# Attention followed by a low-rank mixer: two sets of TensorE transposes replaced by crossbar DMA, u^T in tiles, and the sequence mixer one step later

## The chip, the cores and the metric

The kernel runs on one core of one Trainium2 chip. The metric is device time in microseconds (us). PE is TensorE's matmul part, PEld its weight loads, DVE is VectorE, ACT ScalarE, POOL GpSimd, SP SyncE (here it only issues DMAs). A run over 1.5% above the fastest of its kernel is called slow and left out of the ratios.

## The reference, cut to what matters

```python
# q, k, v: (8 batches, 8 heads, 576 tokens, 64); causal attention with a decay bias from cumsum(max(s, 0))
x  = attention(q, k, v, s)                  # (8, 576, 512)
h  = x.transpose(0, 2, 1) @ U @ V           # low-rank mix over the tokens, rank 32
u  = x + h.transpose(0, 2, 1)               # "sequence mixer"
out = u + np.maximum(u @ w_ch1, 0) @ w_ch2  # "channel mixer", 512 -> 2048 -> 512
```

## The kernel before: the parts that matter

Attention runs over 32 steps `n`, each of two heads of one batch (4 steps a batch). The work is written as Python generators. At each `yield` of an attention or sequence-mixer generator, the driver inserts one piece of channel mixer as *filler* for TensorE. One channel-mixer group has 512 tokens and 32 pieces; a piece is four matmuls of 512 columns. `pace` skips some of the slots.

The sequence mixer of one batch computes `U^T x`, casts it on DVE, and then accumulates, per 128 channels, the transposed x (identity matmuls) and `V^T (U^T x)` into the same tile of PSUM (the memory that matmuls write), so that u^T comes out:

```python
def seqmix(b):                               # cut
    for t in range(5): matmul(up, lhsT=U_sb[:, t, :], rhs=x_sb[:, t, :])
    nc.vector.tensor_copy(ux, up)            # 128x512 cast; the V matmuls need it
    yield
    for dt in range(4):
        for t in range(4):                   # x transposed on TensorE
            matmul(ut[:, ds(t*128, 128)], lhsT=x_sb[:, t, ds(dt*128, 128)], rhs=identity, ...)
        matmul(ut, lhsT=ux[:, ds(dt*128, 128)], rhs=V_sb[:, 0:512], ...)
        copy(uT[:, dt, ds(b*S, 512)], ut)
        yield
    ...                                      # the last 64 tokens, in the same way
def chanmix(g):                              # cut
    for nf in range(16): ...                 # 4 matmuls of 512 columns, ReLU on ACT, yield
    for i in range(4):
        ...                                  # 16 matmuls of 512 columns into f2, yield after each 4
        for dt in range(4):                  # residual: u back to token rows on TensorE
            matmul(f2[:, ds(dt*128, 128)], lhsT=uT[:, dt, ds(tok, 128)], rhs=identity, ...)
        nc.vector.tensor_copy(o_sb, f2)      # then stored
for n in range(PB, NP + 1):                  # the main loop; PB = 4, NP = 32
    ...                                      # transposes(n+1), scores(n), values(n-1), each with filler
        if hp == 0:                          # first step of batch b: mixer of batch b-1
            run(seqmix(b - 1)); fill.append(chanmix(b - 1)); pace[1] = 7   # 7 of 8 slots filled
```

The softmax here doesn't subtract the row's maximum and nothing guards it: scores larger than these inputs give would overflow.

## Time and profile before

The first lines are from the profile's page: the busy table, and the chain of waits that ended last.

```profile
PE 394.9 (96%) x3659; PEld 229.0 (56%) x3659; DVE 222.7 (54%) x445; ACT 199.6 (49%) x384; POOL 56.5 (14%) x79
...
PE 84%; DVE 5%; DMA 4%; ACT 4%; POOL 1%; issue 1%; ACTq 0%
PE pwork L399 30%; PE pwork L412 28%; PE pscore L252 9%; PE pwork L313 6%; PE pwork L231 3%; DMA v_slot_102<-in_v_dram 2%; PE pwork L336 2%; PE pwork L423 2%; PE pwork L357 2%; PE pwork L349 2%; DMA slot_94<-rows_hbm 1%; DVE x_sb L323 1%; PE pscore L149 1%; POOL v_slot_102 L190 1%; DMA hT<-in_s_dram 1%
```

TensorE has nearly all of the span and 84% of the chain. The identity matmuls, L423 (residual) and L349 (x transposed), stand with 2% each on the chain. The next lines are the stretch view, from one sequence mixer's start to the next: length, busy time (and count) of PE, PEld, DVE, ACT and POOL, granted TensorE clock (1.00 is full speed), DMA share (the time of all packets over that of 16 engines; it can pass 1), GB/s.

```profile
129.59:172.59 43.00, 43.00 (x437) 25.67 (x435) 28.23 (x54) 22.09 (x44) 5.88 (x7) 1.00 0.77 69
172.59:215.56 42.97, 42.97 (x436) 25.62 (x434) 27.65 (x54) 22.08 (x44) 5.88 (x7) 1.00 0.70 69
```

PE has no idle time at all there, at full clock. What leaves PE's queue leaves the span, as long as no other wait takes its place.

What does an identity matmul cost? The group table gives 219 ns for each, but matmuls overlap in the pipeline. Start times are the better measure. The timeline (start, length, engine, line, operation, count) at the end of the span:

```profile
401.64 1.67 PE L412 MATMUL pwork<-w_sb,hT 128*128 128x512 bf16 x7
403.15 0.39 PE L423 MATMUL pwork<-identity,uT 128*128 128x128 bf16 x4
403.37 3.62 PE L412 MATMUL pwork<-w_sb,hT 128*128 128x512 bf16 x16
406.82 0.39 PE L423 MATMUL pwork<-identity,uT 128*128 128x128 bf16 x4
```

Four identity matmuls hold PE from 403.15 to 403.37, 0.22 us; sixteen of 512 columns take 3.45 us, 215.6 ns each. The Trainium skill ("TensorE: Matmul & The Clock Gate", section "Wait — 56ns, not 53.3ns?") has N/2.4 GHz + 2.5 ns start to start once the clock is warm, 55.6 and 215.7 ns for 128 and 512 columns. This trace agrees. I use that below as the *slot* of a matmul (at least 25 ns), and call what is left between two starts a *gap*.

### The profile page before, as it was taken

Reading aid. Unit: us, or ns where it says so; the run is one execution under the profiler, and the core shown is the slowest. Engines: PE = TensorE matmul, PEld = TensorE weight load, DVE = VectorE, ACT = ScalarE, POOL = GpSimd, SP = SyncE. Lnnn points to the kernel's source line nnn. Section 1 sums busy time; section 2 is a strip of 40 time slices with the busy share of each in tenths; the row PEclk is TensorE's granted clock in tenths of the full one; section 3 lists DMA queues with packets and bytes.
Section 4 is the critical chain, followed back from the end, with each engine's and each line's share of the span. In section 5 each row is a group of like instructions: output and inputs, shape, how many; then the busy total and the mean of one; then the engine's idle time right before and its main releaser. Section 6 shows DMA issues by size and latency. Waiting matters only on the chain.

```text
span 411.3 us, 8682 instructions
## 1 busy us (share of the span) xinstructions
PE 394.9 (96%) x3659; PEld 229.0 (56%) x3659; DVE 222.7 (54%) x445; ACT 199.6 (49%) x384; POOL 56.5 (14%) x79
## 2 busy tenths in 40 slices
PE   7798989989999999999999999999999999999996
PEld 3475446646565566555655556555656555444442
DVE  7774036866665666665667556676656544002011
ACT  5552688526742574338631873078416830530610
POOL 6750053200500050005000310000000000000000
PEclk9759999999999999999999999999999999999999
DMA  5999999950891059103921195000010001001002
GB/s 75 167 209 208 150 133 122 150 68 29 102 103 54 28 77 128 46 34 48 130 59 53 24 144 66 27 30 3 26 53 27 2 27 51 27 26 56 23 26 77
DMA packets 59301, 29.68 MB, mean 72 GB/s; under 512 B 42302, under 2 KB 53598, under 8 KB 59262
## 3 DMA queue, kind: packets, MB, share of 16 engines
q0 software_dynamic: 53360, 18.44, 62.9%
q1 hardware_dynamic: 5902, 10.69, 7.6%
q8 instruction: 28, 0.46, 0.5%
q14 instruction: 11, 0.09, 0.1%
HBM read 37.51 MB, written 9.95 MB: 115 GB/s over the span
## 4 chain that ended last, share of the span: by engine, by line
PE 84%; DVE 5%; DMA 4%; ACT 4%; POOL 1%; issue 1%; ACTq 0%
PE pwork L399 30%; PE pwork L412 28%; PE pscore L252 9%; PE pwork L313 6%; PE pwork L231 3%; DMA v_slot_102<-in_v_dram 2%; PE pwork L336 2%; PE pwork L423 2%; PE pwork L357 2%; PE pwork L349 2%; DMA slot_94<-rows_hbm 1%; DVE x_sb L323 1%; PE pscore L149 1%; POOL v_slot_102 L190 1%; DMA hT<-in_s_dram 1%
## 5 line engine op out<-in xcount | busy, mean ns | idle before, releaser
L406 ACT ACTIVATE hT<-pwork 128x512 bf16<-128x512 f32 x144 | 88.1, 612 | 133.5 <-PE pwork L399 132.6
L412 PE MATMUL pwork<-w_sb,hT 128*128 128x512 bf16 x576 | 143.2, 379 | 0.2 <-DMA q_sd<-in_q_dram 0.2
L399 PE MATMUL pwork<-uT,w_sb 128*128 128x512 bf16 x576 | 141.0, 379 | 0.5 <-ACT slot_96 L237 0.3
L412 PEld LDWEIGHTS <-hT 128*128 128x128 bf16 x576 | 52.0, 98 | 46.5 <-issue 0.3
L399 PEld LDWEIGHTS <-w_sb 128*128 128x128 bf16 x576 | 51.0, 98 | 46.4 <-issue 0.7
L432 DVE COPY o_sb<-pwork 128x512 f32<-128x512 f32 x36 | 24.9, 692 | 65.4 <-PE pwork L423 65.2
L263 ACT ACTIVATE pT_86<-pscore 128x512 bf16<-128x512 f32 x32 | 19.3, 604 | 32.9 <-PE pscore L252 32.8
L323 DVE TENSOR_TENSOR x_sb<-pwork,rec 128x320 bf16<-128x320 f32 x64 | 31.4, 491 | 2.1
L97 POOL DMA_DIRECT2D q_sd<-in_q_dram x10 | 8.3, 827 | 164.1 <-PE pwork L231 148.2
L366 DVE CAST uT<-pwork 128x512 bf16<-128x512 f32 x30 | 20.5, 690 | 14.2 <-PE pwork L357 14.2
L322 DVE RECIPROCAL rec<-pwork 128x5 f32<-128x5 f32 x64 | 12.3, 192 | 24.7 <-PE pwork L313 24.5
L237 DVE COPY slot_96<-pwork 64x576 bf16<-64x576 bf16 x22 | 17.4, 797 | 13.6 <-PE pwork L231 13.3
L264 DVE TENSOR_TENSOR pT_86<-pT_86,keep 128x512 bf16<-128x512 bf16 x32 | 13.3, 415 | 20.7 <-ACT pT_86 L263 20.7
L264 DVE TENSOR_TENSOR pT_87<-pT_87,keep 128x512 bf16<-128x512 bf16 x32 | 13.2, 415 | 20.1 <-ACT pT_87 L263 20.0
L276 ACT ACTIVATE pT_86<-pscore 128x512 bf16<-128x512 f32 x32 | 19.5, 611 | 5.2 <-PE pscore L252 5.1
L263 ACT ACTIVATE pT_87<-pscore 128x512 bf16<-128x512 f32 x32 | 19.4, 607 | 5.3 <-PE pscore L252 5.2
L231 PEld LDWEIGHTS <-q_sd 72*128 72x128 bf16 x256 | 15.8, 100 | 11.1 <-DMA q_sd<-in_q_dram 0.9
L313 PEld LDWEIGHTS <-pT_87 128*128 128x128 bf16 x480 | 18.8, 100 | 5.6 <-DVE pT_87 L289 0.4
L237 DVE COPY slot_93<-pwork 64x576 bf16<-64x576 bf16 x26 | 20.6, 797 | 1.7 <-PE pwork L231 1.2
L231 PE MATMUL pwork<-identity,k_sd 72*128 72x72 bf16 x256 | 19.1, 201 | 2.2 <-DVE pT_86 L289 1.3
L313 PEld LDWEIGHTS <-pT_86 128*128 128x128 bf16 x480 | 18.5, 100 | 4.5 <-issue 0.6
L276 ACT ACTIVATE pT_87<-pscore 128x512 bf16<-128x512 f32 x32 | 19.6, 612 | 2.9 <-PE pscore L252 2.8
(98 smaller groups left out, 480.2 us busy)
## 6 DMA issues: line engine op xcount, KB each, us to landing
out_dram<-o_sb SPq DMA_DIRECT2D x36, 256.0 KB
w_sb<-in_moe_w_ch_dram POOLq DMA_DIRECT2D x2, 2048.0 KB, 20.6
q_sd<-in_q_dram POOLq DMA_DIRECT2D x7, 576.0 KB, 8.8
k_sd<-in_k_dram POOLq DMA_DIRECT2D x7, 576.0 KB, 12.6
v_slot_102<-in_v_dram POOLq DMA_DIRECT2D x12, 128.0 KB, 13.0
v_slot_103<-in_v_dram POOLq DMA_DIRECT2D x12, 128.0 KB, 13.1
v_slot_104<-in_v_dram POOLq DMA_DIRECT2D x8, 128.0 KB, 12.6
rows_hbm<-hT SPq DMA_DIRECT2D x1, 504.0 KB
```

Source lines behind the costliest of these rows:

```text
L231: nc.tensor.transpose(tp[:, c, t2, :], src[:, h, ds(t2 * 128, 128)], identity[:TP, :TP])
L237: copy(dst[:, :, :, :, par], tp[par * D : par * D + D].rearrange("p c t m -> p c m t"),)
L252: nc.tensor.matmul(dst, lhsT=kT[:, ds(j * 128, 128)], rhs=qT[:, lo:hi], start=True, stop=True,)
L263: nc.scalar.activation(pT[:, hh, 0:512], diag, EXP, scale=scale)
L264: nc.vector.tensor_tensor(pT[:, hh, 0:512].rearrange("p (a b) -> p a b", a=4), pT[:, hh, 0:512].rearrange("p (a b) -> p a b", a=4), keep.t ...
L276: nc.scalar.activation(pT[:, hh, 512:1024], far, EXP, scale=scale)
L313: nc.tensor.matmul(po[:, i, :], lhsT=pT[:, hh, ds(place(j, i), 128)], rhs=vt[:, j, h, :], start=(j == 0), stop=(j == i), skip_group_check= ...
L323: nc.vector.tensor_tensor(x_sb[:, :, ds(h * D, D)], po[:, :, 0:D], rec.to_broadcast([128, 5, D]), op=ALU.mult,)
L399: nc.tensor.matmul(f1, lhsT=w1_sb[:, kt, ds(nf * 128, 128)], rhs=uT[:, kt, ds(g * 512, 512)], start=(kt == 0), stop=(kt == 3),)
L406: nc.scalar.activation(hT[:, nf, :], f1, RELU)
L412: nc.tensor.matmul(f2, lhsT=hT[:, nf, ds(i * 128, 128)], rhs=w2_sb[:, nf, :], start=(nf == 0), stop=False, skip_group_check=True,)
L432: nc.vector.tensor_copy(o_sb, f2)
```

## The change

The intent: take the x transposes (batches 2 to 7) and all residual matmuls off TensorE. Both transposes go to the DMA crossbar (a DMA that transposes while it copies); the additions join PSUM evacuations that DVE does anyway. For that, u^T is kept in one tile per token group, x is stored by head pair, and from batch 2 on the mixer runs one step later, to give the last transpose of a batch time to land. The diff, cut to its core:

```diff
+    FT = 2
-    uT = consts.tile([128, 4, B * S], BF16)
+    def uT(g): ...  # work.tile([128, 4, 512], BF16, tag="uT", bufs=4), one per token group
 def values(n):
-            x_of[b] = work.tile([128, 5, DM], BF16, ...)
+            x_of[b] = work.tile([128, PB, 5, 128], BF16, ...)
+            if b >= FT: xT_of[b] = work.tile([128, 4, 640], BF16, tag="xT", bufs=1)
...
+            if hh == 1 and b >= FT:
+                nc.sync.dma_start_transpose(
+                    out=xT_of[b][:, hp, :].rearrange("p (t m) -> p t m", t=5),
+                    in_=x_sb[:, hp, :, :].rearrange("p t d -> p (t d)"))
 def seqmix(b):
+        def evac(dt, lo, hi, src):           # cut where a token group ends
+            if xT is not None: nc.vector.tensor_tensor(dst, src, xT[:, dt, lo:hi], op=ALU.add)
+            ...                              # else a copy, as before
...                                          # identity matmuls only if xT is None
 def chanmix(g):
+        u_sd = work.tile([128, 4, 4, 128], BF16, tag="u_sd")
+        nc.sync.dma_start_transpose(out=u_sd..., in_=u...)    # 512 KB, all of the group
...
-            for dt in range(4): nc.tensor.matmul(f2[:, ds(dt * 128, 128)], lhsT=uT[...], rhs=identity, ...)
-            nc.vector.tensor_copy(o_sb, f2)
+            nc.vector.tensor_tensor(o_sb..., f2..., u_sd[:, :, i, :], op=ALU.add)
 main loop
-    for n in range(PB, NP + 1):
+    for n in range(PB, NP + 2):
...
+        if hp == 1 and b > FT:
+            run(seqmix(b - 1))
+            fill.append(chanmix(b - 1))
-            if hp == 0:
+            if hp == 0 and b <= FT:
```

More of the change, by code (lines that the diff above doesn't have):

```diff
@@ L210, with uT @@
     load_v(1)
-    uT = consts.tile([128, 4, B * S], BF16)
-    x_of = {}
+    uT_of, x_of, xT_of = {}, {}, {}
+    def uT(g):
+        if g not in uT_of:
+            uT_of[g] = work.tile([128, 4, 512], BF16, tag="uT", name="uT", bufs=4)
+        return uT_of[g]
     def transposes(n):
@@ L305, in values @@
         if hp == 0:
-            x_of[b] = work.tile([128, 5, DM], BF16, tag="x_sb", name="x_sb")
+            x_of[b] = work.tile([128, PB, 5, 128], BF16, tag="x_sb", name="x_sb")
+            if b >= FT:
+                xT_of[b] = work.tile([128, 4, 640], BF16, tag="xT", name="xT", bufs=1)
         x_sb, pT, vt = x_of[b], pTs[n % 2], v_slots[b % 3]
@@ L323, in values @@
             nc.vector.tensor_tensor(
-                x_sb[:, :, ds(h * D, D)],
+                x_sb[:, hp, :, ds(hh * D, D)],
                 po[:, :, 0:D],
@@ L328, in values @@
             )
+            if hh == 1 and b >= FT:
+                nc.sync.dma_start_transpose(
+                    out=xT_of[b][:, hp, :].rearrange("p (t m) -> p t m", t=5),
+                    in_=x_sb[:, hp, :, :].rearrange("p t d -> p (t d)"),
+                )
             yield
@@ L338, in seqmix @@
                 lhsT=U_sb[:, t, :],
-                rhs=x_sb[:, t, :],
+                rhs=x_sb[:, :, t, :],
                 start=(t == 0),
@@ L345, in seqmix @@
         yield
+        xT = xT_of.pop(b, None)
+        cut = 512 - 64 * b
+        def evac(dt, lo, hi, src):
+            g, at = (b, 64 * b + lo) if lo < cut else (b + 1, lo - cut)
+            dst = uT(g)[:, dt, at : at + hi - lo]
+            if xT is not None:
+                nc.vector.tensor_tensor(dst, src, xT[:, dt, lo:hi], op=ALU.add)
+            elif b == 0 and type(dt) is int and dt % 2:
+                nc.scalar.copy(dst, src)
+            else:
+                nc.vector.tensor_copy(dst, src)
         for dt in range(4):
             ut = pwork()
-            for t in range(4):
+            if xT is None:
+                for t in range(4):
+                    nc.tensor.matmul(
+                        ut[:, ds(t * 128, 128)],
+                        lhsT=x_sb[:, dt, t, :],
+                        rhs=identity,
+                        start=(t == 0),
+                        stop=False,
+                        skip_group_check=True,
+                    )
+            nc.tensor.matmul(
+                ut,
+                lhsT=ux[:, ds(dt * 128, 128)],
+                rhs=V_sb[:, 0:512],
+                start=(xT is not None),
+                stop=True,
+                skip_group_check=True,
+            )
+            evac(dt, 0, cut, ut[:, 0:cut])
+            if cut < 512:
+                evac(dt, cut, 512, ut[:, cut:512])
+            yield
+        ut = pwork()[:, 0:256].rearrange("p (a b) -> p a b", a=4)
+        for dt in range(4):
+            if xT is None:
                 nc.tensor.matmul(
-                    ut[:, ds(t * 128, 128)],
-                    lhsT=x_sb[:, t, ds(dt * 128, 128)],
-                    rhs=identity,
-                    start=(t == 0),
+                    ut[:, dt, :],
+                    lhsT=x_sb[:, dt, 4, :],
+                    rhs=identity[:, :64],
+                    start=True,
                     stop=False,
@@ L357, in seqmix @@
             nc.tensor.matmul(
-                ut,
+                ut[:, dt, :],
                 lhsT=ux[:, ds(dt * 128, 128)],
-                rhs=V_sb[:, 0:512],
-                start=False,
+                rhs=V_sb[:, 512:S],
+                start=(xT is not None),
                 stop=True,
@@ L364, in seqmix @@
             )
-            copy = nc.scalar.copy if b == 0 and dt % 2 else nc.vector.tensor_copy
-            copy(uT[:, dt, ds(b * S, 512)], ut)
-            yield
-        ut = pwork()
-        for dt in range(4):
-            nc.tensor.matmul(
-                ut[:, ds(dt * 64, 64)],
-                lhsT=x_sb[:, 4, ds(dt * 128, 128)],
-                rhs=identity[:, :64],
-                start=True,
-                stop=False,
-                skip_group_check=True,
-            )
-            nc.tensor.matmul(
-                ut[:, ds(dt * 64, 64)],
-                lhsT=ux[:, ds(dt * 128, 128)],
-                rhs=V_sb[:, 512:S],
-                start=False,
-                stop=True,
-                skip_group_check=True,
-            )
-        nc.vector.tensor_copy(
-            uT[:, :, ds(b * S + 512, 64)], ut[:, 0:256].rearrange("p (a b) -> p a b", a=4)
-        )
+        evac(slice(0, 4), 512, S, ut)
         yield
@@ L395, in chanmix @@
         hT = work.tile([128, NF, 512], BF16, tag="hT", name="hT")
+        u = uT_of.pop(g)
+        u_sd = work.tile([128, 4, 4, 128], BF16, tag="u_sd", name="u_sd")
+        nc.sync.dma_start_transpose(
+            out=u_sd.rearrange("p a b c -> p (a b) c"), in_=u.rearrange("p a b -> p (a b)")
+        )
         for nf in range(NF):
@@ L401, in chanmix @@
                     lhsT=w1_sb[:, kt, ds(nf * 128, 128)],
-                    rhs=uT[:, kt, ds(g * 512, 512)],
+                    rhs=u[:, kt, :],
                     start=(kt == 0),
@@ L409, in chanmix @@
             f2 = pwork()
-            tok = g * 512 + i * 128
             for nf in range(NF):
@@ L416, in chanmix @@
                     start=(nf == 0),
-                    stop=False,
-                    skip_group_check=True,
+                    stop=(nf == NF - 1),
                 )
@@ L421, in chanmix @@
                     yield
-            for dt in range(4):
-                nc.tensor.matmul(
-                    f2[:, ds(dt * 128, 128)],
-                    lhsT=uT[:, dt, ds(tok, 128)],
-                    rhs=identity,
-                    start=False,
-                    stop=(dt == 3),
-                    skip_group_check=True,
-                )
-            o_sb = work.tile([128, DM], FP32, tag="o_sb", name="o_sb", bufs=3)
-            nc.vector.tensor_copy(o_sb, f2)
-            nc.sync.dma_start(out=out_flat[ds(tok, 128), :], in_=o_sb)
+            o_sb = work.tile([128, DM], FP32, tag="o_sb", name="o_sb", bufs=3)
+            nc.vector.tensor_tensor(
+                o_sb.rearrange("p (a b) -> p a b", a=4),
+                f2.rearrange("p (a b) -> p a b", a=4),
+                u_sd[:, :, i, :],
+                op=ALU.add,
+            )
+            nc.sync.dma_start(out=out_flat[ds(g * 512 + i * 128, 128), :], in_=o_sb)
             yield
@@ L498 @@
             run(scores(n))
-        if n > PB:
+        if hp == 1 and b > FT:
+            run(seqmix(b - 1))
+            fill.append(chanmix(b - 1))
+        if PB < n <= NP:
             run(values(n - 1))
-            if hp == 0:
+            if hp == 0 and b <= FT:
                 run(seqmix(b - 1))
@@ L504 @@
                 pace[1] = 7
+    pace[1] = 8
     fill.append(chanmix(NG - 1))
-    pace[1] = 8
     while fill:
```

## The prediction

> **What bounds it now.** TensorE: in the busy table PE has 96% of the span, DVE 54%, ACT 49%; the chain of waits is 84% PE. In the stretches between sequence mixers (129-172, 172-215 us) PE is busy 43.0 of 43.0 us at clock 1.00, so each removed slot of PE issue should come off the span.
>
> **Removed from PE** (start to start in the timeline, since one matmul's 219 ns overlaps its neighbours):
> - The residual: 4 identity matmuls of 128 columns per output tile take 0.22-0.23 us (395.79 to 396.02). 36 tiles: 8.1 us.
> - The transposes of x, batches 2-7: 16 of 128 columns (4 x 0.225 us) and 4 of 64 (half of 0.23 us), 1.0 us a batch: 6.1 us.
>
> Together 14.2 us, all on the chain: 400.6 us if nothing else changed.
>
> **Added.**
> - DVE: evacuations become adds. The tensor_tensor of 320 columns takes 491 ns, the 512-column copy 692 ns; I estimate an add of 512 near 0.69 us too. An evacuation across a group's edge is cut in two, 0.16 us more: some 28 cuts, 4-5 us. DVE is at 28 of 43 us per batch, off the chain.
> - DMA: 24 transposes of 160 KB and 9 of 512 KB, on the SP queue. The Trainium skill gives 1309 ns for 128x128 ("VectorE: DVE Perf Modes", The three transpose paths) and 261 GB/s ("DMA: Bandwidth & Descriptors", Latency and other measured facts). Estimates from these: 6.5 or 0.6 us for x, 21 or 2 us for u; this trace has no transpose. Slack: a batch's last x transpose is issued about 9 us before its add; u's has 16 first-layer steps of 0.87 us and 3.45 us of second layer, 17 us. Both should mostly hide, though they meet load bursts (DMA row of the page at 90%), where a small row load took 6 us.
>
> **A new bubble.** I counted the generators' steps. The channel mixer supplies 32 filler steps per batch; mixers one step later need about 7 more once. Where mixer 2 now runs, chanmix(1) is just used up, and all six mixer steps run unfilled (before: one or two). PE then shows the latency: ux's cast and hop 0.95 us, then four split adds of about 0.85 us that group 2's first matmul awaits: about 3 us idle, once, near 135-140 us. Waits of mixers for x_sb (2.4 us in all) mostly stay, being in batches 0 and 1.
>
> **Sum.** 414.8 - 14.2 + 3 (bubble) - 0.5 + 0.5 (transpose waits) = about 403.5 us, range 399.5 to 409. Faster by over 2%: 0.70; within 2%: 0.25; slower: 0.05.
>
> **What would show it.**
> - PE busy down 13-15 us, matmuls 3659 to 3395.
> - PE idle 2-4 us before group 2's first layer, released by DVE; elsewhere between 150 and 340 us PE busy over 98%.
> - DVE's waits for a DMA at the mixer's add or at o_sb: under 2 us in total; more means slow transposes.
> - Mixer-to-mixer period from 43 to about 41 us.
> - After the last mixer, second-layer tiles 3.45 us apart instead of 3.68.
>
> **What would make it wrong.** Transposes near 1.3 us per block, one after another, would keep the DMA engines busy over 300 us, delay q, k, v and stall PE (over 409 us). The SP queue is in order: a transpose waiting for x, or behind a store, could hold back row loads that the scores need. A smaller bubble would give 400.

## More of the kernel before

In the rounds after the prediction the kernel before took 414.9 us (median of 4 runs).

Last, a mixer in the timeline, for comparison with later ones:

```profile
302.44 1.24 PE L336 MATMUL pwork<-x_sb,U_sb 128*128 128x512 bf16 x5
303.52 1.03 PE L412 MATMUL pwork<-w_sb,hT 128*128 128x512 bf16 x4
304.38 0.39 PE L349 MATMUL pwork<-identity,x_sb 128*128 128x128 bf16 x4
304.61 0.38 PE L357 MATMUL pwork<-V_sb,ux 128*128 128x512 bf16 x1
```

Between the U matmuls and the first V matmul, which needs the cast ux, there are a filler piece (L412) and four identity matmuls (L349): enough work to hide the cast.

## The result

The changed kernel takes 403.12 us (median of 4 runs, 402.07 to 404.34). The ratio of the mean times of the runs of both kernels in the same rounds (so not quite the ratio of the medians) is 0.9724, interval 0.9687 to 0.9762: faster by 2.8%. A second time, in other rounds, it was 0.9732. The page after, the same parts:

```profile
PE 381.6 (95%) x3395; PEld 213.8 (53%) x3395; DVE 223.8 (56%) x473; ACT 200.5 (50%) x384; POOL 56.6 (14%) x79
...
PE 76%; DMA 11%; DVE 6%; ACT 3%; issue 1%; POOL 1%; DVEq 0%; ACTq 0%
```

The 264 identity matmuls are gone and PE is busy for 13.3 us less. DMA's larger share of the chain is no new steady wait: 31.0 us of it are one load of k that ends at 53.8 us, and PE's waits for a DMA are all in the first 55 us, in code that is the same in both kernels. The stretches from mixer to mixer:

```profile
173.30:214.78 41.48, 41.44 (x398) 23.70 (x397) 28.00 (x59) 22.54 (x46) 5.88 (x7) 1.00 0.89 100
214.78:256.75 41.97, 41.18 (x398) 23.57 (x397) 28.49 (x58) 22.20 (x45) 5.89 (x7) 1.00 0.85 98
256.75:297.85 41.10, 41.10 (x399) 23.59 (x398) 28.20 (x58) 21.95 (x45) 0.00 (x0) 1.00 0.29 57
```

A batch takes 41 to 42 us instead of 43. After the last mixer, output tiles follow without the residual (timeline):

```profile
340.52 13.98 PE L432 MATMUL pwork<-uT,w_sb 128*128 128x512 bf16 x64
354.33 13.98 PE L444 MATMUL pwork<-w_sb,hT 128*128 128x512 bf16 x64
368.14 13.98 PE L432 MATMUL pwork<-uT,w_sb 128*128 128x512 bf16 x64
```

Four output tiles now take 368.14 - 354.33 = 13.81 us, 3.45 each; before it was 3.67 (403.15 to 406.82 in the earlier timeline). And this is the mixer of batch 2, the first that is delayed (timeline; the brackets are the idle time before, and what ended it):

```profile
133.57 1.24 PE L349 MATMUL pwork<-x_sb,U_sb 128*128 128x512 bf16 x5
135.60 1.04 PE L385 MATMUL pwork<-V_sb,ux 128*128 128x512 bf16 x4 [0.79 <-DVE ux L357]
136.84 0.29 PE L408 MATMUL pwork<-V_sb,ux 128*128 128x64 bf16 x4 [0.20 <-DVE uT L367]
137.51 0.63 PE L321 MATMUL pwork<-v_slot_102,pT_86 128*128 128x65 bf16 x15 [0.37 <-DVE uT L367]
138.17 1.04 PE L432 MATMUL pwork<-uT,w_sb 128*128 128x512 bf16 x4
```

No filler (L444 or L432) stands between its parts. From start times the gaps are 0.95 + 0.37 + 0.54 + 0.20 = 2.06 us.

Because PE's matmuls start one after another in the trace, the span can be added up exactly. I take the part from the start of mixer 1 to the end (the part before it is nearly the same code and varies by 2 to 3 us for another reason, below). Mixer 1 starts here, before and after:

```profile
86.82 1.24 PE L336 MATMUL pwork<-x_sb,U_sb 128*128 128x512 bf16 x5 [1.34 <-DVE x_sb L323]
86.32 1.24 PE L349 MATMUL pwork<-x_sb,U_sb 128*128 128x512 bf16 x5 [1.34 <-DVE x_sb L331]
```

In us, from the start times (my sums, not a view of the profile):

| | mixer 1 starts | from there to the end | slots | gaps | last matmul to end |
|---|---|---|---|---|---|
| before | 86.8 | 324.5 | 316.9 | 3.3 | 4.2 |
| changed | 86.3 | 314.1 | 303.5 | 6.0 | 4.6 |
| changed, second profile | 85.8 | 314.1 | 303.5 | 6.0 | 4.6 |

So 13.4 us of slots left after mixer 1 (and 0.7 before it, 14.1 in all), 2.7 us of new gaps came, of which 2.06 at mixer 2, and 0.4 at the tail.

The transposes themselves, from the trace's DMA records and the issue times (us; my reading, not a view of the profile):

```
                      issue to first packet   first packet to last   landing after issue
x, no load running    1.2                     0.95                   2.1 to 2.2 (one: 4.2)
x, just after a u     1.5 to 1.8              0.9                    2.3 to 2.7
x, in a load burst    1.2 to 4.4              2.3 to 4.1             3.5 to 8.2
u, groups 1 to 8      1.2 to 1.4              2.6                    3.7 to 4.0
u, group 0 (at 41)    4.3                     10.1                   14.4
```

How long each transpose kept the SP queue, and the add that takes u in (ns: shortest/median/longest; then first and last start in us):

```profile
L338 SPq DMA_TRANSPOSE xT<-x_sb x24: 1199/1211/1758, 101.7 to 324.5; - x24
L426 SPq DMA_TRANSPOSE u_sd<-uT x9: 1853/2154/8005, 41.0 to 341.8; - x9
L454 DVE TENSOR_TENSOR o_sb<-pwork,u_sd x36: 691/692/693, 65.2 to 396.0; 128x512 f32<-128x512 f32 x36
```

### The profile page after: what moved, and what is told of

Read it like the earlier page. It is cut to its first block, busy times and chain, and to the rows that moved or that the text cites. A ratio compares the mean times of both kernels' runs of the same rounds, so it can differ in the third digit from the quotient of the medians.

```text
span 400.4 us, 8275 instructions
## 1 busy us (share of the span) xinstructions
PE 381.6 (95%) x3395; PEld 213.8 (53%) x3395; DVE 223.8 (56%) x473; ACT 200.5 (50%) x384; POOL 56.6 (14%) x79
## 4 chain that ended last, share of the span: by engine, by line
PE 76%; DMA 11%; DVE 6%; ACT 3%; issue 1%; POOL 1%; DVEq 0%; ACTq 0%
PE pwork L444 28%; PE pwork L432 28%; PE pscore L258 8%; DMA k_sd<-in_k_dram 8%; PE pwork L321 6%; PE pwork L237 3%; DMA v_slot_102<-in_v_dram 2%; PE pwork L349 2%; PE pwork L385 2%; DVE slot_96 L243 1%; DVE slot_95 L243 1%; DMA hT<-in_s_dram 1%; DVE x_sb L331 1%; DVE ux L357 1%; DVE o_sb L454 1%
## 5 line engine op out<-in xcount | busy, mean ns | idle before, releaser
L444 PE MATMUL pwork<-w_sb,hT 128*128 128x512 bf16 x576 | 141.3, 379 | 0.2 <-ACT slot_96 L243 0.2
L432 PE MATMUL pwork<-uT,w_sb 128*128 128x512 bf16 x576 | 141.0, 379 | 0.4 <-ACT slot_96 L243 0.3
L444 PEld LDWEIGHTS <-hT 128*128 128x128 bf16 x576 | 52.3, 98 | 50.1 <-issue 0.3
L432 PEld LDWEIGHTS <-w_sb 128*128 128x128 bf16 x576 | 51.0, 98 | 46.9 <-issue 0.4
L454 DVE TENSOR_TENSOR o_sb<-pwork,u_sd 128x512 f32<-128x512 f32 x36 | 24.9, 692 | 63.4 <-PE pwork L444 62.2
L367 DVE TENSOR_TENSOR uT<-pwork,xT 128x256 bf16<-128x256 f32 (+6 forms) x54 | 19.8, 418 | 6.1 <-PE pwork L385 6.1
```

Of the source, the lines that this page charges most:

```text
L432: nc.tensor.matmul(f1, lhsT=w1_sb[:, kt, ds(nf * 128, 128)], rhs=u[:, kt, :], start=(kt == 0), stop=(kt == 3),)
L444: nc.tensor.matmul(f2, lhsT=hT[:, nf, ds(i * 128, 128)], rhs=w2_sb[:, nf, :], start=(nf == 0), stop=(nf == NF - 1),)
L454: nc.vector.tensor_tensor(o_sb.rearrange("p (a b) -> p a b", a=4), f2.rearrange("p (a b) -> p a b", a=4), u_sd[:, :, i, :], op=ALU.add,)
```

## The experiments

All twelve were compared with the kernel before in the same rounds, five rounds each (six runs of a kernel with the profiled one, five of "doubled but group 0"); all give the correct result. My theory was: the gain is PE slots removed, less the latency of mixers that find no filler. Rivals: the gain comes from the later mixer or from the tiles; the delay is needed for the DMA; the DMA is near its limit.

| kernel | median us (before) | ratio, 95% interval |
|---|---|---|
| tiles only | 413.66 (413.62) | 1.0009 (0.9978-1.0040) |
| residual only | 406.18 (413.62) | 0.983 (0.9799-0.986) |
| no delay | 403.03 (413.62) | 0.9744 (0.9717-0.977) |
| slower filler in batch 2 | 401.42 (413.62) | 0.9699 (0.9672-0.9726) |
| changed, again | 403.41 (415.06) | 0.9732 (0.9692-0.9772) |
| x only | 410.42 (415.06) | 0.9909 (0.9873-0.9945) |
| delay only | 414.57 (415.06) | 1.0001 (0.9966-1.0035) |
| transposes doubled | 409.61, fast runs (415.06) | 0.9857 (0.9803-0.9911) |
| even filler | 403.79 (413.21) | 0.9758 (0.9718-0.9798) |
| doubled but group 0 | 402.50 (413.21) | 0.9745 (0.9719-0.9771) |
| even filler, x from batch 1 | 405.22 (413.21) | 0.9821 (0.9781-0.9861) |
| even filler from batch 2 | 400.80 (413.71) | 0.9682 (0.9656-0.9707) |

### One part at a time

Tiles only: `FT = 8` (no x by DMA, no delay) and the residual back on TensorE.

```diff
-    FT = 2
+    FT = 8
-        nc.sync.dma_start_transpose(out=u_sd..., in_=u...)
+            for dt in range(4): nc.tensor.matmul(f2[:, ds(dt*128, 128)], lhsT=u[:, dt, ds(i*128, 128)], rhs=identity, ...)
```

> Only u^T in tiles per token group and x by head pair; all transposes and the residual on TensorE, mixers where they were. Theory 1: the same matmuls as before, so 414.8 us within 1 us (the cut evacuations are off the chain). Rival (the single u^T tile of before caused false waits): under 412.5 us.

Measured: the same as before, and 324.5 us from mixer 1 to the end, as before. The tiles and the cut evacuations are neutral.

Residual only: `FT = 8` alone.

> Only the residual goes through the DMA; x is transposed on TensorE in all batches and no mixer is delayed. Theory 1 (the gain is removed PE issue slots, 0.421 ns a column): 144 x 128 columns leave, 7.8 us, so about 407.0 us beside 414.8 before. Rival (the gain comes from the mixer one step later, or from splitting u^T into tiles, and the transposes are about neutral): between 413 and 415 us, since no mixer moved.

Measured 406.18, 7.4 us less. In the profile the stretch after mixer 1 fell from 324.5 to 317.8: slots -7.4, gaps +0.8, the tail the same within 0.1. Rivals that put the gain into the tiles or the delay fall here.

x only: the residual back on TensorE, the rest as changed.

> Only x goes through the DMA, with the mixers one step later; the residual stays on TensorE. Theory 1: 13,824 columns leave, 5.8 us, and the delay gives back 1.5 to 2 us: about 409.5 us beside 413.6. Rival (x's transposes cost as much in waits as they free): 412 us or more.

Measured 410.42, where the kernel before had 415.06 (by the means, 0.9909, it is 3.8 us; its interval leaves out 1). After mixer 1: 321.1 us, slots -6.1, gaps +2.6. So the new gaps come with this half. Both halves add up: 324.5 - 317.8 = 6.7 and 324.5 - 321.1 = 3.4 make 10.1, and the whole change gives 10.4.

Delay only: the tiles, all on TensorE, and mixers 2 to 7 one step later.

```diff
-    FT = 2                                   # and the residual back on TensorE
+    FT = 8
-        if hp == 1 and b > FT:
+        if hp == 1 and b > 2:
-            if hp == 0 and b <= FT:
+            if hp == 0 and b <= 2:
```

> Only the delay of mixers 2 to 7 by one step, everything on TensorE. Theory 1: no matmul leaves, filler is missing once at mixer 2: 1 to 2 us slower than the kernel before, 415 us beside 413.6, with PE gaps of about 2 us near mixer 2. Rival (the delay is itself a gain, since the mixer no longer waits for the newest x): faster than before by 1 us or more.

Measured: no difference (1.0001), and only 0.5 us more gaps after mixer 1. My number was too high. I had put the whole bubble down to missing filler, but in this kernel the mixers still carry the identity matmuls of x, which cover part of the latency: the gap before the first V matmul of mixer 2 is 0.73 us here and 0.95 without them, which differs by their four slots of 0.056 us. The delay alone opens 0.73 + 0.12 + 0.19 = 1.04 us at mixer 2, and closes 0.5 us of gaps elsewhere. The 2.06 us take both: with the delay the filler runs out at mixer 2, and with the transposes gone the mixer has less of its own to put there.

### Is the delay worth having?

```diff
-        if hp == 1 and b > FT:
-            run(seqmix(b - 1))
-            fill.append(chanmix(b - 1))
-            if hp == 0 and b <= FT:
+            if hp == 0:
```

> The changed kernel, but every mixer stays where it was before (no step of delay). Theory 1: the last x transpose of a batch lands about 2 us after its issue and the add that needs it comes 4 us or more after, so nothing waits; mixer 2 has its filler again and its 2.05 us of PE gaps go: about 401 us beside 403. Rival (the delay is needed to hide the transposes): DVE waits for the DMA at the fourth add of each mixer and PE stalls, several us in all: 405 us or more.

Measured 403.03, ratio 0.9744: no different from the changed kernel. My 401 was wrong, and so was the rival. The bubble at mixer 2 is gone, but the gaps after mixer 1 sum to 5.5 us (changed: 6.0, before: 3.3): other mixers now meet a skipped slot or used-up filler, 0.95 us at the mixer at 256 us and 1.0 us around the one at 213 us. DVE does wait for the transposes, briefly (waits, total, times, longest):

```profile
DVE uT L367 <- DMA xT<-x_sb: 1.9, 4, 0.5
```

In the changed kernel this line doesn't occur. So the delay hides 1.9 us of short DVE waits, and in the end the gaps only move: 0.5 us of difference in the stretch after mixer 1. Most of the new gaps (2.2 of 2.7 us) are there without the delay too: they come with the removed matmuls, and the delay decides where they lie.

### Is the bubble a lack of filler?

From mixer 1 to mixer 2 the filler is slowed, so that some is left.

```diff
-                pace[1] = 7
+                pace[1] = 6 if b == FT else 7
...                                          # and pace[1] = 7 after the first delayed mixer
```

> The changed kernel with the filler slowed from 7 to 6 of 8 steps from mixer 1 to mixer 2, so that about 3 filler pieces are left for mixer 2 when it runs one step later. Theory 1 (the bubble is lack of filler): gaps of 2.05 us at mixer 2 shrink to under 1 us, no new gaps elsewhere, about 401.5 us. Rival (the bubble is the wait for the transposed x, whatever the filler): the gaps and 403 us stay.

Measured 401.42. Mixer 2 in its timeline:

```profile
131.82 1.24 PE L349 MATMUL pwork<-x_sb,U_sb 128*128 128x512 bf16 x5
132.90 1.03 PE L444 MATMUL pwork<-w_sb,hT 128*128 128x512 bf16 x4
133.84 0.39 PE L385 MATMUL pwork<-V_sb,ux 128*128 128x512 bf16 x1
134.07 1.03 PE L444 MATMUL pwork<-w_sb,hT 128*128 128x512 bf16 x4
```

Filler stands where PE was idle, the gaps after mixer 1 are 4.0 instead of 6.0 us, and the stretch takes 312.1 instead of 314.1. The bubble at mixer 2 was lack of filler; the transposed x was not what PE waited for. (The verdict is the profile's: the intervals of the ratios, 0.9699 and 0.9732, overlap. The 0.95 us at mixer 4 stay.)

### How much slack do the transposes have?

Each transpose is issued twice, the copy into a tile that nobody reads.

```diff
-        nc.sync.dma_start_transpose(out=u_sd..., in_=u...)
+        for dst in (u_sd, u_sd2):
+            nc.sync.dma_start_transpose(out=dst..., in_=u...)
...                                          # and the same for xT, into a scratch tile xT2
```

> The changed kernel with each transpose issued twice, the second into a tile that nobody reads: 8.65 MB of crossbar traffic more. Theory 1 (the transposes have slack): within 1 us of the changed kernel; an x transpose with its copy lands within 5 us when no load burst runs. Rival (the transposes are near the limit of the DMA engines or of the in-order SP queue, and loads or row loads come late): 2 us slower or more, with PE or DVE waits for a DMA.

Measured 405.9 to 414.0 us; three of the six runs count as slow, and the median of the other three is 409.61. The rival seemed right. But in its profile all the loss is before mixer 1, which starts at 94.4 us instead of 86.3; the stretch after it takes 313.5 us, no longer than the changed kernel's 314.1. The timeline between 68 and 82 us, where PE waits for DMA:

```profile
68.57 0.28 PE L322 MATMUL pwork<-v_slot,pT 128*128 128x65 bf16 x4 [1.96 <-DMA v_slot<-in_v_dram]
70.63 0.44 PE L322 MATMUL pwork<-v_slot,pT 128*128 128x65 bf16 x5 [1.78 <-DMA v_slot<-in_v_dram]
72.02 1.06 PE L322 MATMUL pwork<-v_slot,pT 128*128 128x65 bf16 x16 [0.96 <-DMA v_slot<-in_v_dram]
81.65 0.30 PE L237 MATMUL pwork<-identity,k_sd 72*128 72x72 bf16 x4 [1.27 <-DMA k_sd<-in_k_dram]
```

PE waits for batch 1's v and batch 2's k, 6.0 us in all, where the changed kernel has no wait for a DMA after 55 us; and from 69.8 to 76.6 us TensorE is granted half its clock. Group 0's u is transposed at 41 us, inside the load of the weights; its copy landed only at 68.8 us (DMA records). The next kernel doubles everything except group 0:

```diff
+        for dst in (u_sd, u_sd2)[: 2 if g > 0 else 1]:
```

> As the kernel with doubled transposes, but group 0's u is transposed only once. Theory 1 (doubling costs only because u of group 0 is transposed at 41 us, inside the weights' load, and holds up batch 1's v loads; later there is slack): mixer 1 starts at 86 to 88 us again instead of 94.4, about 403 us. Rival (doubled transposes cost in every batch): 408 us or more as before.

Measured 402.5, mixer 1 at 86.7 us, 313.6 us from there on: as the changed kernel. So 8 MB of crossbar traffic more costs nothing once the weights are loaded, and one 512 KB transpose more, inside the load, costs 7.7 us in these two profiles. The single transpose of group 0 in the changed kernel costs nothing that can be seen: its mixer 1 starts at 86.3 us, where the kernel before, with 0.7 us of slots more, has 86.8. (This trace lacks 55 matmul records, so its gaps can't be summed.)

### Spreading the filler evenly

Every mixer step gets a piece; the other steps share what is left: 0.28 pieces per step in batch 1 (before 3/8), 0.68 in batch 2, then 0.8.

```diff
+    def step_fill(always=False):
+        if not always:
+            pace[0] += pace[1]
+            if pace[0] < 1: return
+            pace[0] -= 1
...
+            run(seqmix(b - 1), True)
```

> The changed kernel with the filler spread evenly: every mixer step always gets a piece, the other steps get 0.28 (batch 1), 0.68 (batch 2) and 0.8 pieces each. Theory 1 (what the change gives back is mixer latency without filler): the PE gaps at mixers 2 to 7 go (2.05 + 0.37 + 0.95 + 0.16 us in the changed kernel), the stretch from mixer 1 to the end falls from 314.1 to about 311 us, about 0.967 of the kernel before. Rival (filler is only moved, and gaps open where it is missing): the sum of gaps after mixer 1 stays at 9.4 us and the ratio at 0.973.

Measured 403.79, scattered from 401.2 to 406.1: no gain. From mixer 1 on it took 313.6 us and not 311, though some filler was only moved there: 93 filler matmuls are recorded before mixer 1, where the changed kernel has 116 (this trace lacks 58 of 3395 matmul records, which explains a few of the 23). The loss is before mixer 1, which starts at 88.8 us. Two stretches of this kernel:

```profile
56.00:59.90 3.90, 2.31 (x26) 1.45 (x26) 1.60 (x3) 3.80 (x6) 2.10 (x3) 1.00 3.41 112
59.90:70.20 10.30, 9.88 (x83) 6.74 (x85) 3.83 (x10) 7.79 (x16) 1.23 (x2) 0.50 2.43 137
```

The clock column reads 0.50: after a stretch with PE busy 2.31 of 3.90 us, TensorE was granted half its clock for 10 us, three times 3.4. In the changed kernel the same stretch, and a thin one at mixer 2, kept the full clock:

```profile
56.00:59.90 3.90, 2.84 (x25) 1.57 (x24) 1.14 (x2) 3.80 (x7) 2.51 (x3) 1.00 3.17 111
133.90:137.80 3.90, 2.54 (x23) 0.97 (x21) 2.92 (x7) 0.80 (x2) 0.00 (x0) 1.00 0.21 74
```

Sparse filler in batch 1 is the likely cause. But the busy share alone doesn't decide: the kernel before and the one with slower filler have the same pace up to here and are both busy for 2.80 of 4.00 us, and only the second loses its clock (first the kernel before, then slower filler):

```profile
58.00:62.00 4.00, 2.80 (x38) 1.98 (x36) 0.92 (x4) 3.93 (x9) 1.56 (x2) 1.00 1.73 152
62.00:66.00 4.00, 4.00 (x34) 2.35 (x31) 2.36 (x6) 3.88 (x8) 0.00 (x0) 1.00 3.56 122
58.00:62.00 4.00, 2.80 (x32) 1.85 (x31) 0.92 (x3) 3.93 (x8) 2.00 (x3) 0.99 2.39 109
62.00:66.00 4.00, 4.00 (x25) 2.06 (x23) 2.21 (x5) 2.98 (x6) 0.44 (x1) 0.59 1.81 169
```

The Trainium skill ("TensorE: Matmul & The Clock Gate", section "What's actually happening") tells of a monitor that halves the clock after an idle window of about 3.4 us. The length agrees (in the clock records of all these traces, the stretches between two changes last whole multiples of 3.41 us), but the longest gap here was 1.9 us. That a thinly used window did it, and that it depends on where the windows happen to begin in a run, is argued and not shown.

The same effect fits the scatter of these kernels. A half-clock stretch of 3.4 us that begins at 61.9 to 62.3 us stands in the profiles of some (residual only, no delay, delay only, slower filler: mixer 1 at 88.0 to 88.6 us) and not of others (before, changed, tiles only, x only: 85.8 to 87.1); half of 3.4 us is 1.7. Whole runs of the kernel before fall into two groups, at clock 0.983 mostly 412.3 to 413.7 us, at 0.975 414.6 to 415.6; where in those runs the clock fell was not recorded.

Moving x to the DMA from batch 1 on was tried on top:

```diff
-    FT = 2
+    FT = 1                                   # the delay still begins at mixer 2
```

> The even filler, and x by DMA from batch 1 on instead of batch 2 (mixer 1 stays undelayed). Theory 1: 1.0 us of PE slots leave, and four transposes more fall into 55 to 86 us, where the DMA engines are still loading weights and batch 2; the fifth to eighth of them may land late, so between 1 us faster and 2 us slower than the even filler alone; if slower, a DVE wait for x's transpose or a PE wait for q, k or v before mixer 1 shows it. Rival (early DMA has slack as well): a clean gain of 1 us.

Measured 405.22, 1.4 us above the even filler. The intervals of the two ratios overlap, so that the medians alone don't show a loss; in the profiles (this one of a run of 408.37 us, among the slowest) the stretch from mixer 1 on takes 317.0 us instead of 313.6. Its waits show why:

```profile
DVE uT L367 <- DMA xT<-x_sb: 5.7, 2, 3.7
```

Here the transposes do come late, because they fall into the loads, and PE then waits 2.4 us for DVE from 98.9 us on and has half its clock for 3.4 us after that.

The last kernel leaves everything up to mixer 1 as it was, and spreads the filler evenly only after it.

```diff
-                pace[1] = 7
+                rate[1] = 0.68
...                                          # 0.8 after the first delayed mixer; mixer steps always filled
```

> The changed kernel untouched up to mixer 1, then the even filler (every mixer step gets a piece; 0.68 per other step in batch 2, 0.8 after). Theory 1: the even filler was right for mixers 2 to 7 and lost only in batch 1, where too little filler let PE's granted clock fall to half for 10 us. So mixer 1 starts at 86 to 88 us as in the changed kernel, the stretch from it to the end is 310 to 311.5 us against 314.1, and the whole is 0.965 to 0.969 of the kernel before, about 399.5 us beside 413.5. Rival (filler spread evenly costs as much elsewhere): the stretch stays over 313 us.

Measured 400.8 us (400.44 to 401.19), ratio 0.9682, the best of all; mixer 1 at 87.2 us, then 311.6 us, just over the expected 310 to 311.5. Its gaps after mixer 1 are 3.5 us, about the 3.3 of the kernel before. Against the slower filler (0.9699) the intervals overlap, so that the last step is not shown; against the changed kernel (0.9732) they overlap by a hair, and the profiles, 2.5 us apart in the stretch that repeats to 0.1 us, carry the verdict.

The first rerun of the changed kernel:

> The changed kernel as it is, timed in the rounds of the three others. Removed 32,256 columns at 0.421 ns are 13.6 us, the gaps at mixers rise by about 2 us: 11.5 us under the kernel before, so 402 us if that has 413.6 again.

Measured 403.41 beside 415.06, 11.65 us less.

## Why the prediction was right

- **PE slots.** Predicted 14.2 us; the start times give 14.1. The chain was PE, and residual and x by themselves gave 7.4 and 4.6 us in medians, so the slots did come off the span (in the stretch after mixer 1, net of new gaps, 6.7 and 3.4).
- **The bubble.** Predicted about 3 us, once, at 135 to 140 us. Measured 2.06 us of gaps between 134.7 and 138.2, plus 0.95 us at mixer 4, which the prediction didn't have. The evacuations were oversized: nine adds took 3.1 us, and PE had value matmuls to put beside them. New gaps after mixer 1 sum to 2.7 us, close to the 3 of the sum, partly by luck. The prediction named only filler as the cause; the delay alone opens 1.0 us at mixer 2 (0.5 in sum), and the rest comes because the removed matmuls had covered latency too.
- **DVE.** An add of 512 columns takes 692 ns, as estimated. DVE's busy time rose by 1.1 us, where 4 to 5 were predicted. An evacuation cut in two is dearer (549 + 285 ns against 692), but the two overlap in the records. Nothing depended on it.
- **DMA.** For x 0.6 to 6.5 us were predicted, and it landed after 2.1 us in quiet and after up to 8.2 in load bursts, outside the range. For u 2 to 21 held: 3.8 us in quiet, 14.4 inside the first load. The rate of the "DMA: Bandwidth & Descriptors" page was the better guide (160 KB in 0.95 us is 172 GB/s, 512 KB in 2.6 us is 202), not the 1309 ns per 128x128 of "VectorE: DVE Perf Modes" (0.19 and 0.16 us per block here). Added to the 1.2 us before the first packet, 0.19 us would make 1.4 us for one block alone, an estimate near that page's figure: it can't be multiplied by the number of blocks. DVE never waited for a DMA at the adds, under the 2 us allowed.
- **Signs.** 3395 matmuls, PE busy down 13.3 us, period 41.1 to 42.0 us, output tiles 3.45 us apart, PE busy 189.2 of 190 us from 150 to 340: all as predicted (the last tells nothing, since the kernel before has the same 189.2). PE's idle time before group 2's first layer, 2 to 4 us predicted, is 2.06 by the start times and 1.36 by the brackets.
- **The sum.** 403.5 predicted, 403.1 measured. The terms that can be checked were each right within 1 us (what its -0.5 stands for it doesn't say). Slots, gaps and tail as measured would give 414.9 - 14.1 + 2.7 + 0.4 = 403.9. That the total met within 0.4 us is partly luck, since single runs of the changed kernel lie between 402.1 and 404.3.

## What to carry to other kernels

On a kernel whose first engine is full, count slots from start to start, not busy times, and then ask what the removed work was hiding: identity matmuls were also cover for a cast's latency, and filler has to be steered to that place. Here a crossbar transpose was close to free after the first loads, when issued a few us ahead, and one more inside the load of the weights cost 7.7 us. Check filler changes against the granted clock: here it fell to half after thin stretches, though not after every one.

## What the Trainium skill lacked or had wrong

- "TensorE: Matmul & The Clock Gate", section "Back-to-back issue gap", gives sustained spacings of about 81 ns (128 columns) and 131 ns (512) for streams of weight loads and matmuls. Here such streams ran at 55 to 56 and 215.6 ns, which is that page's other formula.
- The same page, in its table "Why this matters for your kernels", warns of PE idle gaps above about 3 us; of shorter idle times it says only that frequent ones can do the same. Here the clock fell to half for 10.2 us after gaps of at most 1.9 us, with PE busy 2.31 of 3.90 us, and stayed full with 2.54 of 3.90 at mixer 2. How busy a window must be, no page states and no run here settles.
- "VectorE: DVE Perf Modes", section "The three transpose paths": 1309 ns for a 128x128 block by crossbar DMA, without saying how much of it is paid once. In DMAs of 5 and 16 blocks it was 0.19 and 0.16 us per block, after 1.2 us from issue to first packet.
- "DMA: Bandwidth & Descriptors" has the time that a transpose holds its issuing queue only in a comparison made for trn3, in cycles and for other sizes. Here it was 1.21 us for 160 KB and 2.15 us for 512 KB in the median (8.0 us in the first load), where a plain 256 KB store held it mostly for 0.33 to 0.37 us. No page has how a transpose slows down among loads: 3.5 to 8.2 us to land instead of 2.1 for 160 KB, 14.4 instead of 3.8 for 512 KB.
